# Attention products in 64x64 TensorE tiles, the causal mask moved to VectorE, and a reordered opening, in a DeltaNet and cosine-router kernel

## The chip, the cores and the metric

The kernel runs on one core of one Trainium2 chip. The metric is device time in microseconds of one execution, the median over repeated runs. The profile shows one execution; the times in its rows are counted from the first instruction of that execution.

A core has five engines that run their own instruction streams and wait for each other through semaphores: TensorE (PE in the profile, with its weight loads listed as PEld), VectorE (DVE), ScalarE (ACT), GpSimd (POOL) and SyncE (SP, which here mostly issues DMAs).

## The reference

The first half is a delta-rule linear attention over 4 batches, 8 heads, 768 positions and a head size of 48. The second half is a router that sends each of the 3072 tokens (384 wide, the 8 heads side by side) to one of 8 experts, a two-layer network of width 1024.

```python
k_n = k / (norm(k) + 1e-6)
for t in range(S):
    y[:, :, t] = einsum('bhd,bhde->bhe', q[:, :, t], state)
    v_old = einsum('bhde,bhd->bhe', state, k_n[:, :, t])
    state = state + beta[:, :, t] * einsum('bhd,bhe->bhde', k_n[:, :, t], v[:, :, t] - v_old)
x = y.transpose(0, 2, 1, 3).reshape(B * S, H * D)
logits = (x / norm(x)) @ (emb / norm(emb)).T / tau
e = argmax(logits); gate = softmax(logits)[e]
out = gate * (relu(x @ w1[e]) @ w2[e])
```

All of it is float32.

## The kernel before, in words

**Tiling of the attention.** Positions are cut into 12 chunks of 64 (`m`), and batches into two pairs (`i`). One chunk of one batch pair is a *unit* (`n`, 24 in all); it holds 16 heads as 8 pairs. Inside a chunk the recurrence becomes a triangular system: the kernel builds the Gram matrix of the keys, inverts the 32x32 diagonal blocks of it, and solves for the chunk's updates in two half steps (`solve`, `fix`, `solve_again`), then updates the state (`update`, `new_state`) and forms the output (`from_state`, `inside`). A unit's small products are written with `four(f)`: for each of 4 head pairs, the four corners of the TensorE array, so that one step is 16 calls of `mm`.

**Groups and preparation.** The inverses are made for a *group* of two chunks (four units) at a time, in `prepare(g)`, six groups in all. Its steps: load keys, square and sum them (`square`, `total`), root and scale factors (`roots`, `scales`), scaled keys (`keys`), transpose them (`transposes`, evicted by `out_of_psum`), Gram blocks of the diagonal (`gram_diag`, 64 products of 32x32 a chunk), bring them to lanes (`to_lanes`, a VectorE transpose out of PSUM), clear the upper part (`lower`, GpSimd), then 30 pairs of VectorE operations (`product`, `subtract`, L485 and L489) that do the inversion in every lane at once, `from_lanes`, and `spread` (ScalarE), which writes `W`, the operand of `solve`.

**Per unit, beside the solves.** `gram` (16 products of 64x96) gives the scores; `corner` and `scores` evict them on ScalarE, and `causal` (L582, GpSimd) multiplies them with a mask. After the output, `transposes` (L706) and `xT_out` turn the tokens' rows, `logits` multiplies them with the expert embeddings, and every four units `routing` picks experts, assigns places (`places`), and writes tokens and lists to DRAM.

**Order of the work.** Nothing is in program order by hand: every step is a task for `Plan`, with an engine, an assumed busy time, a due time `key`, and what it reads and writes. `Plan.order` plays the tasks through with these assumed times and emits each engine's stream in the resulting order; on the chip each engine then runs its stream strictly in that order. PSUM is four pairs of banks that tasks take and give back; in `before`, each task that gives a pair back names it with `give`.

**Expert stage.** After the plan, a second part works through the tokens in tiles of 128: `transposed`, `hidden` (L1090), `result` (L1097), with the experts' weights streamed from DRAM. Two such tiles of the first expert (`early_tile`) are already in the plan, late in it.

**Other lines that are named below.** L245 and L248 are the helpers `mm` and `act_copy`, through which most TensorE products and ScalarE evictions go, so they are told apart by tile names. `L432` and `L521` are the transposes of keys and queries, `L470` is `to_lanes`, `L475` is `lower`, `L497` is `from_lanes`, `L600` is `rest`, `L653` and `L651` are `new_state`, `L307` to `L309` load beta.

Of the kernel before, what the change touches and what calls it, by code (L numbers as in the profile page):

```python
# [16 lines left out]
C = 64  # L17
# [5 lines left out]
PERIOD = 7.5  # L23


class Plan:

    def __init__(self, psum):
        self.tasks, self.last, self.readers, self.psum, self.held = [], {}, {}, psum, {}

    def add(self, engine, busy, more, key, run, reads=(), writes=(), take=None, give=None):
        i, after = len(self.tasks), set()
        if take:
            writes = list(writes) + [("psum", take)]
        for r in reads:
            after.update(self.last.get(r, ()))
            self.readers.setdefault(r, []).append(i)
        for w in writes:
            after.update(self.last.get(w, ()))
            after.update(self.readers.pop(w, ()))  # L40
            self.last[w] = [i]
        after.discard(i)
        self.tasks.append((engine, busy, busy + more, key, run, after, take, give))

    def order(self):
# [7 lines left out]
        now, events, serial = 0.0, [], 0  # L53
# [3 lines left out]
        self.span = 0.0  # L57
        self.load = {}
        while len(order) < n:
            for e in sorted(waiting):  # L60
# [5 lines left out]
                i = min(can, key=lambda i: (self.tasks[i][3], i))  # L66
                waiting[e].remove(i)
                _, busy, whole, _, _, _, take, give = self.tasks[i]
                free -= bool(take)
                order.append((now, i))  # L70
                idle[e] = now + busy
# [4 lines left out]
                serial += 2  # L76
            if len(order) == n:
                break
            now = events[0][0]
            while events and events[0][0] <= now + 1e-9:  # L80
                _, _, i = heapq.heappop(events)
                if i < 0:
                    continue
                free += bool(self.tasks[i][7])
                for j in then[i]:
                    missing[j] -= 1
                    ready[j] = max(ready[j], now)
                    if not missing[j]:
                        waiting.setdefault(self.tasks[j][0], []).append(j)
        return order  # L90

    def emit(self):
        free = list(range(len(self.psum)))
        for _, i in self.order():
            _, _, _, _, run, _, take, give = self.tasks[i]
            if take:
                self.held[take] = free.pop(0)
            run()
            if give:
                free.append(self.held[give])  # L100
# [6 lines left out]
def kernel(  # L107
# [22 lines left out]
    WIDE = C  # L130
# [57 lines left out]
    buffers("q", 2, [2, H, WIDE])  # L188
    buffers("v", 3, [2, H, D])
    buffers("sq", 1, [2, H, D])  # L190
    buffers("K", 6, [2, H, WIDE])
# [3 lines left out]
    buffers("rt", 2, [2, 2, NP, 2])  # L195
    rings["X"], rings["WT"] = carved(2, [HC, HC], w2_flat), carved(3, [HC, HC], w2_flat)[2:]
# [45 lines left out]
    HALF = (slice(0, C), slice(C, 2 * C))  # L242

# [9 lines left out]
    half = cpool.tile([128, 2 * GROUP * H], F32, name="half")  # L253
    root = ac.tile([128, 1], F32, name="root")
    bt = rings["XC"][0].rearrange("p g r -> p (g r)")[0:40, 0:NM * 2 * C].rearrange("p (m o t) -> p m o t", m=NM, o=2)
    bt_odd = rings["XC"][1].rearrange("p g r -> p (g r)")[0:40, 0:NM * 2 * C].rearrange("p (m o t) -> p m o t", m=NM, o=2)
# [14 lines left out]
    def pairs_of_heads(t, i, j):  # L271
        return t[:, i, 2 * j:2 * j + 2].rearrange("p h d -> p (h d)")

    def start_constants():
        nc.vector.memset(half, 0.5)
# [6 lines left out]
        for t in rings["K"] + rings["q"]:  # L284
            nc.gpsimd.memset(t[:, :, :, D:WIDE], 0.0)
# [17 lines left out]
    def load_beta():  # L303
        for i in range(2):
            for o in range(2):
                b = beta[2 * i + o].rearrange("(j jj) (m t) -> jj j m t", jj=2, t=C)
                nc.sync.dma_start(out=bt[i * NP:(i + 1) * NP, :, o], in_=b[0])  # L307
                nc.sync.dma_start(out=bt[32 + i * NP:32 + (i + 1) * NP, :, o], in_=b[1])
                nc.sync.dma_start(out=bt_odd[32 + i * NP:32 + (i + 1) * NP, :, 1 - o], in_=b[1])  # L309

    def beta_transposes():
        p = pair("beta")
        for m in range(NM):
            for x, (t, r) in enumerate(((bt, 0), (bt, 32), (bt_odd, 32))):
                nc.tensor.transpose(p[:, min(x, 1), (3 * m + x) * 8:(3 * m + x + 1) * 8],
                                    t[r:r + 8, m].rearrange("p o t -> p (o t)"), ident[r:r + 8, r:r + 8])

    def beta_out():
        p = pair("beta")[:, :, 0:NM * 24].rearrange("p b (m x c) -> p b m x c", x=3, c=8)
        flat = beta_s.rearrange("p m x i j -> p m x (i j)")  # L320
        nc.vector.tensor_copy(flat[:, :, 0], p[:, 0, :, 0])
        nc.vector.tensor_copy(flat[:, :, 1:3], p[:, 1, :, 1:3])

    def newton(r, b, q_):
        nc.vector.tensor_scalar_max(r, r, 1e-30)
        nc.vector.reciprocal(q_, r)
        nc.vector.tensor_tensor(q_, q_, b, op=ALU.mult)
        nc.vector.tensor_tensor(r, r, q_, op=ALU.add)
        nc.vector.tensor_scalar_mul(r, r, 0.5)

    def beta_root(part):
        def step():
            nc.scalar.activation(sqb[:, part], beta_s[:, part], ACT.Sqrt)
        return step

    def beta_newton(part):
        return lambda: newton(sqb[:, part], beta_s[:, part], quot[:, part])
# [6 lines left out]
    def planned_k(m, key):  # L344
        for i in range(2):
            e = nc.scalar if m < 2 and i else nc.sync
            plan.add("ACT" if m < 2 and i else "SP", 2.0, 2.2, key + 0.1 * i,
# [10 lines left out]
    def prepare(g):  # L358
        ms = (2 * g, 2 * g + 1)
        t0 = group_key(g)  # L360
        for m in ms:
            planned_k(m, t0 - 14 * PERIOD + (m % 2) * 2 * PERIOD if m > 1 else -200.0 + m)
        if g == 0:
            plan.add("SP", 1.5, 2.5, -150.0, load_beta, writes=["bt"])
            plan.add("DVE", 1.0, 0.2, -100.0, masks, reads=["iotas"], writes=["masks"])
            plan.add("PE", 2.5, 0.3, -140.0, beta_transposes, reads=["bt", "ident"], take="beta")
            plan.add("DVE", 0.6, 0.2, -140.0, beta_out, reads=[("psum", "beta")], writes=["beta_s"], give="beta")
            for part in (slice(0, 2), slice(2, NM)):
                plan.add("ACT", 0.4, 0.2, -140.0, beta_root(part), reads=["beta_s"], writes=[("sqb", part.start)])
                plan.add("DVE", 1.5, 0.2, -139.0, beta_newton(part), reads=["beta_s"], writes=[("sqb", part.start), "quot"])  # L370
        root_part = ("sqb", 0 if g == 0 else 2)
# [16 lines left out]
        both = [at("rn", g) + (0,), at("rn", g) + (1,)]  # L388
        flat, flat_rt = (t.rearrange("p m i j jj -> p (m i j jj)") for t in (ss, rt))

        def roots():
            nc.gpsimd.tensor_tensor(out=flat_rt, in0=flat, in1=half[:, 0:32], op=ALU.pow)

        def roots_act():
            nc.scalar.activation(flat_rt, flat, ACT.Sqrt)

        def roots_newton():
            nc.vector.tensor_scalar_max(flat_rt, flat_rt, 1e-30)
            nc.vector.tensor_scalar_max(flat, flat, 0.0)
            q_ = quot[:, 0:2].rearrange("p a b c d -> p (a b c d)")[:, 0:32]  # L400
            nc.vector.reciprocal(q_, flat_rt)
            nc.vector.tensor_tensor(q_, q_, flat, op=ALU.mult)
            nc.vector.tensor_tensor(flat_rt, flat_rt, q_, op=ALU.add)
            nc.vector.tensor_scalar_mul(flat_rt, flat_rt, 0.5)
        if g < 2:
            plan.add(*act(32), t0 - 10 * PERIOD, roots_act, reads=both, writes=[at("rt", g)])
            plan.add("DVE", 1.2, 0.2, t0 - 10 * PERIOD, roots_newton, reads=both, writes=[at("rt", g), "quot"])
        else:
            plan.add("POOL", 5.5, 0.2, t0 - 10 * PERIOD, roots, reads=both + ["half"], writes=[at("rt", g)])

        def scales():
            nc.vector.tensor_scalar_add(flat_rt, flat_rt, 1e-6)
            nc.vector.reciprocal(flat_rt, flat_rt)
            for m in ms:
                nc.vector.tensor_tensor(rt[:, m % 2], rt[:, m % 2],
                                        sqb[:, m, 0:3:2].rearrange("p jj i j -> p i j jj"), op=ALU.mult)
        plan.add("DVE", 0.7, 0.2, t0 - 9.6 * PERIOD, scales, reads=[root_part], writes=[at("rt", g)])

        def keys(m):
            def step():  # L420
                for i in range(2):
                    (nc.vector if m == 1 else nc.gpsimd).tensor_tensor(
                        buf("K", m)[:, i, :, 0:D], buf("k", m)[:, i],
# [3 lines left out]
        def transposes(src, m, name):  # L427
            def step():
                p = pair((name, m))
                for i in range(2):  # L430
                    for j in range(NP):
                        nc.tensor.transpose(p[:, i, j * 128:(j + 1) * 128], pairs_of_heads(buf(src, m), i, j), ident)  # L432
            return step

        def out_of_psum(m, name, cols):
            def step():
                act_copy(buf("KQ", m).rearrange("d i j y c -> d (i j y) c")[:, :, cols],
                         pair((name, m)).rearrange("d i (x c) -> d (i x) c", c=C))
# [785 lines left out]
```

## Time and profile before

| What | us |
|---|---|
| median of 14 runs (lowest 661.88, highest 678.58) | 669.91 |
| the profiled execution, its own time | 671.66 |
| its span, first to last instruction | 669.9 |
| first `solve` starts (tile `V`,`W`) | 89.14 |
| fifth `places` starts (tile `run`,`ones`) | 319.61 |
| first TensorE instruction of the expert stage | 368.17 |

The mean granted TensorE clock over the span is 0.868. In the page, "issue" as the reason of an idle time means that the engine waited for nothing that the profile shows. A timeline row merges neighbouring instructions of a kind: start, length, engine, line, operation, tiles, shapes, how many, and in brackets the idle time before it and what ended it.

### The profile page before, as it was taken

How to read it: one execution, taken by the hardware profiler on the slowest of the kernel's cores; microseconds unless marked ns; L12 is line 12 of the kernel's file. 1: busy time of each engine (PE TensorE's matmuls, PEld its weight loads, DVE VectorE, ACT ScalarE, POOL GpSimd, SP SyncE). 2: the span in 40 equal slices, each digit the busy share in tenths (PEclk: the TensorE clock that was granted, in tenths of full speed). 3: DMA queues.
4: the chain of work that ended last, by engine and by line, in shares of the span. 5: the costliest groups of instructions: out<-in, count | busy, mean ns of one | idle time of the engine just before them, and what ended most of it. 6: DMA issues, size and time to landing. Idle time of an engine off the chain costs nothing. (4 is left out here: it accounts for less than half of the span.)

```text
span 669.9 us, 22522 instructions
## 1 busy us (share of the span) xinstructions
PE 560.6 (84%) x9887; PEld 473.4 (71%) x9887; DVE 275.9 (41%) x715; ACT 177.8 (27%) x350; POOL 195.9 (29%) x223
## 2 busy tenths in 40 slices
PE   0364648988787978888997989999999999999992
PEld 0253548887776867788885867878788787878781
DVE  3848998867868967952215101111111111111100
ACT  2232244733534526554341001101010111111010
POOL 2335352647333343333314111212112121212010
PEclk9986555766778869977899889999999999999997
DMA  4444745441231341031201899999999999999700
GB/s 70 82 76 79 195 73 91 74 111 29 39 89 31 64 144 28 10 95 53 79 27 64 292 390 387 370 329 325 316 337 311 335 320 338 308 328 338 234 23 7
DMA packets 129078, 115.49 MB, mean 172 GB/s; under 512 B 84986, under 2 KB 115105, under 8 KB 128978
## 3 DMA queue, kind: packets, MB, share of 16 engines
q1 hardware_dynamic: 122450, 102.98, 50.4%
q0 software_dynamic: 4352, 10.66, 4.3%
q8 instruction: 79, 1.29, 0.8%
q10 hardware_dynamic: 2176, 0.39, 0.4%
q14 instruction: 21, 0.17, 0.1%
HBM read 102.07 MB, written 12.72 MB: 171 GB/s over the span
## 5 line engine op out<-in xcount | busy, mean ns | idle before, releaser
L1092 ACT ACTIVATE hT<-acc 128x512 f32<-128x512 f32 x52 | 31.1, 597 | 261.3 <-PE acc L1090 261.3
L1090 PEld LDWEIGHTS acc<-xTm,w 128*128 128x128 f32 x816 | 93.8, 192 | 4.5
L1090 PE MATMUL acc<-xTm,w 128*128 128x128 f32 x816 | 93.9, 275 | 0.0
L1097 PE MATMUL acc<-w,hT 128*128 128x384 f32 x272 | 92.2, 493 | 0.0
L1100 POOL DMA_INDIRECT out_dram<-y,ids x26 | 26.4, 1014 | 215.1 <-DVE y L1099 197.9
L489 DVE TENSOR_TENSOR w_first<-w_first,tmp 128x30 f32<-128x30 f32 (+9 forms) x180 | 76.5, 427 | 4.5
L485 DVE TENSOR_TENSOR tmp<-w_first 128x30 f32<-128x30 f32 (+9 forms) x180 | 73.3, 409 | 5.8 <-POOL w_first L475 1.4
L1097 PEld LDWEIGHTS acc<-w,hT 128*128 128x128 f32 x272 | 51.1, 193 | 32.4 <-issue 1.7
L1082 DVE COPY xTm<-acc 128x384 f32<-128x384 f32 x26 | 14.5, 558 | 135.2 <-PE acc L1081 131.5
L1099 DVE TENSOR_SCALAR y<-acc,xg 128x384 f32<-128x384 f32 x26 | 16.1, 618 | 126.7 <-PE acc L1097 126.7
L245 PE MATMUL psum_pair<-KQ 48*32 48x32 f32 (+1 forms) x2304 | 50.6, 247 | 21.0 <-issue 17.4
L245 PEld LDWEIGHTS psum_pair<-KQ 48*32 48x32 f32 (+1 forms) x2304 | 41.5, 137 | 28.0 <-issue 22.4
L1090 PEld LDWEIGHTS acc<-xTm,w_first 128*128 128x128 f32 x432 | 51.2, 197 | 3.2 <-DVE xTm L1082 1.0
L582 POOL TENSOR_TENSOR M<-M,upper 128x512 f32<-128x512 f32 x24 | 31.3, 1305 | 73.7 <-ACT M L248 68.3
L1090 PE MATMUL acc<-xTm,w_first 128*128 128x128 f32 x432 | 51.4, 281 | 0.8 <-DVE xTm L1082 0.8
L1097 PE MATMUL acc<-w_first,hT 128*128 128x384 f32 x144 | 47.9, 486 | 0.0
L245 PE MATMUL psum_pair<-S,KQ 48*64 48x48 f32 x1408 | 36.4, 254 | 4.9 <-DVE lz L717 2.1
L1097 PEld LDWEIGHTS acc<-w_first,hT 128*128 128x128 f32 x144 | 26.7, 190 | 16.7
L245 PEld LDWEIGHTS psum_pair<-S,KQ 48*64 48x64 f32 x1408 | 32.1, 169 | 7.4 <-DVE lz L717 2.3
L248 ACT ACTIVATE KQ<-psum_pair 128x1024 f32<-128x1024 f32 x24 | 24.5, 1023 | 36.6 <-PE psum_pair L245 15.5
L1065 POOL DMA_INDIRECT xg<-x_dram,ids x26 | 25.2, 971 | 30.2 <-DMA ids<-idmap 19.6
L542 POOL TENSOR_TENSOR V<-v,sqb 128x384 f32<-128x384 f32 x24 | 20.6, 864 | 34.3 <-DVE R L600 30.9
(181 smaller groups left out, 772.7 us busy)
## 6 DMA issues: line engine op xcount, KB each, us to landing
w<-in_moe_w_dram SPq DMA_DIRECT2D x34, 1536.0 KB
w_first<-in_moe_w_dram SPq DMA_DIRECT2D x16, 1536.0 KB
q<-in_q_dram SPq DMA_DIRECT2D x96, 48.0 KB
v<-in_v_dram SPq DMA_DIRECT2D x48, 96.0 KB
w_first<-in_k_dram SPq DMA_DIRECT2D x88, 48.0 KB
x_dram<-XC SPq DMA_DIRECT2D x5, 800.0 KB
idmap<-space SPq DMA_DIRECT2D x1, 2048.0 KB
w_first<-in_moe_w_dram SPq DMA_DIRECT2D x6, 256.0 KB
```

The source lines that it names most:

```text
L245: nc.tensor.matmul(out_, lhsT=lhsT, rhs=rhs, start=start, stop=True, skip_group_check=True)
L248: nc.scalar.activation(out_, in_, ACT.Copy, scale=scale)
L485: nc.vector.tensor_tensor(t, X[:, j + 1:, j:j + 1].broadcast_to([128, rows, j]), X[:, j:j + 1, 0:j].broadcast_to([128, rows, j]), op=ALU.mult)
L489: nc.vector.tensor_tensor(X[:, j + 1:, 0:j], X[:, j + 1:, 0:j], t, op=ALU.subtract)
L542: nc.gpsimd.tensor_tensor(buf("V", m)[:, i].rearrange("p jj j d -> p jj (j d)").rearrange("p jj (j d) -> p jj j d", d=D), buf("v", m)[:, i ...
L582: nc.gpsimd.tensor_tensor(M, M, K["upper"].broadcast_to([128, H, C]), op=ALU.mult)
L1065: t.read = nc.gpsimd.indirect_dma_start(out=t.x, out_offset=None, in_=x_dram[:, :], in_offset=bass.IndirectOffsetOnAxis(ap=t.ids[:, 0:1], ...
L1090: nc.tensor.matmul(psH[:, i, :], lhsT=t.w1[:, j, (f + i) * 128:(f + i + 1) * 128], rhs=t.xT[:, j, :], start=(j == 0), stop=(j == KC - 1))
L1092: nc.scalar.activation(t.hT[:, f:f + 4, :], psH, ACT.Relu)
L1097: nc.tensor.matmul(psO, lhsT=t.hT[:, f, :], rhs=t.w2[:, f, :], start=(f == 0), stop=(f == NF - 1))
L1099: nc.vector.tensor_scalar_mul(y, psO, t.x[:, Dm:Dm + 1])
L1100: nc.gpsimd.indirect_dma_start(out=out[:, :], out_offset=bass.IndirectOffsetOnAxis(ap=t.ids[:, 1:2], axis=0), in_=y, in_offset=None, bound ...
```

## The change

1. **Products in 64x64 tiles.** Transposes of keys, queries and tokens were transposes of whole 128x128 blocks; they become `mm` products with a 64x64 identity, four corners each (`turned`). The logits, three products over 128 rows, become 12 over 64 rows in two PSUM halves that VectorE adds. The keys are stored without padding between heads (`heads`), beta is transposed by `mm` too.
2. **The mask.** `scores` (ScalarE) and `causal` (GpSimd) become one VectorE operation from PSUM into `M`.
3. **The opening.** Beta is loaded ahead of the second chunk's keys, with 8 DMAs and no second copy; half of that chunk's keys come through the GpSimd queue; roots are refined in 3 operations where there were 5 or 6, separately for chunk 0 and 1; and tasks of group 0 on VectorE are marked `hold`.
4. **The planner.** `hold` lets an engine wait up to `HOLD` for a more urgent task; `mode` and `STAY` make TensorE prefer tasks of the same tile shape; a PSUM pair is free when its last user has been emitted, counted, in place of a named `give`.
5. `from_lanes` writes contiguously, and `spread` reads with a stride in its place.

The core of the diff:

```diff
-    def add(self, engine, busy, more, key, run, reads=(), writes=(), take=None, give=None):
+    def add(self, engine, busy, more, key, run, reads=(), writes=(), take=None, mode=0, hold=False):
...
-                i = min(can, key=lambda i: (self.tasks[i][3], i))
+                i = min(can, key=lambda i: (self.tasks[i][3] + STAY * (e == "PE" and self.tasks[i][8] != mode_now), i))
+                if any(self.tasks[x][9] and now < ready[x] < now + HOLD and self.tasks[x][3] < self.tasks[i][3]
+                       and now + self.tasks[i][1] > ready[x] + 0.1 for x in waiting[e]):
+                    continue
...
-                free += bool(self.tasks[i][7])
+                for a in self.tasks[i][7]:
+                    left[a] -= 1
+                    free += not left[a]
...
+    def turned(p, t):
+        for i in range(2):
+            for j in range(NP):
+                for jj, y in CORNERS:
+                    c = (2 * j + jj) * D
+                    mm(p[HALF[jj], y, (i * NP + j) * C:(i * NP + j + 1) * C], t[HALF[y], i, c:c + C], ident[HALF[y], HALF[y]])
...
-            e = nc.scalar if m < 2 and i else nc.sync
+            e, name, busy = (nc.sync, "SP", 2.2) if m > 1 or not i else (nc.scalar, "ACT", 2.8) if m == 0 else (nc.gpsimd, "POOL", 4.0)
...
-            nc.vector.transpose(WT.rearrange("p x i -> p i x"), X)
+            nc.vector.transpose(WT, X)
...
-            act_copy(M.rearrange("p (jj j) c -> p jj j c", jj=2), split()[:, :, :, HC:])
-
-        def causal():
-            nc.gpsimd.tensor_tensor(M, M, K["upper"].broadcast_to([128, H, C]), op=ALU.mult)
+            nc.vector.tensor_tensor(M.rearrange("p (jj j) c -> p jj j c", jj=2), split()[:, :, :, HC:],
+                                    K["upper"].unsqueeze(1).broadcast_to([128, 2, NP, C]), op=ALU.mult)
...
             for j in range(KC):
-                nc.tensor.transpose(p[:, 0, j * 128:(j + 1) * 128], xrow[:, j * 128:(j + 1) * 128], ident)
+                for a, o in CORNERS:
+                    c = (2 * j + a) * C
+                    mm(p[HALF[a], o, j * C:(j + 1) * C], xrow[HALF[o], c:c + C], ident[HALF[o], HALF[o]])
...
             for j in range(KC):
-                mm(p, buf("xT", n)[:, j], enT[:, j, :], j == 0)
+                for a, o in CORNERS:
+                    mm(p[HALF[o], a, 0:E], buf("xT", n)[HALF[a], j, o * C:(o + 1) * C], enT[HALF[a], j, :], j == 0)
```

## The prediction

> **What bounds the kernel now.** I read the windows first, cut at the three times in the table: the opening, the units, the tail with the early tiles, the expert stage. Columns: stretch, length, busy time (and count) of PE, PEld, DVE, ACT, POOL, granted clock, DMA share, GB/s.
>
> ```profile
> 0.00:89.00 89.00, 36.34 (x1071) 30.80 (x1071) 62.23 (x152) 22.95 (x32) 33.21 (x57) 0.77 0.49 98
> 89.00:320.00 231.00, 195.28 (x6367) 178.21 (x6367) 169.71 (x443) 108.76 (x223) 97.91 (x96) 0.75 0.30 66
> 320.00:368.00 48.00, 42.96 (x709) 35.10 (x708) 13.45 (x69) 15.06 (x44) 14.89 (x20) 0.96 0.18 59
> 368.00:658.00 290.00, 286.03 (x1742) 229.25 (x1742) 30.56 (x52) 31.06 (x52) 48.89 (x51) 0.99 0.87 305
> ...
> 255.00:270.00 15.00, 13.32 (x538) 12.03 (x538) 12.85 (x34) 9.37 (x21) 4.32 (x4) 1.00 0.17 31
> ```
>
> The expert stage is TensorE at 286 of 290 us and unchanged: whatever the attention gains or loses shows one to one at the end. In the units nothing is full: PE 195 of 231, DVE 170. The page gives the clue:
>
> ```profile
> PE 560.6 (84%) x9887; PEld 473.4 (71%) x9887; DVE 275.9 (41%) x715; ACT 177.8 (27%) x350; POOL 195.9 (29%) x223
> ...
> q8 instruction: 79, 1.29, 0.8%
> ```
>
> 19,774 PE instructions against 79 packets on an instruction queue: some 250 a packet. The PE timeline shows when that counts:
>
> ```profile
> 39.66 1.26 PE L245 MATMUL psum_pair<-KQ 48*32 48x32 f32 x108 [1.53 <-issue]
> 40.85 1.09 PE L432 MATMUL psum_pair<-ident,K 128*128 128x128 f32 x8
> 41.87 0.27 PE L245 MATMUL psum_pair<-KQ 48*32 48x32 f32 x11
> 43.50 1.82 PE L245 MATMUL psum_pair<-KQ 48*32 48x32 f32 x128 [1.35 <-issue]
> 47.78 2.54 PE L245 MATMUL psum_pair<-KQ 48*64 48x96 f32 x128 [2.46 <-issue]
> ...
> 89.14 1.11 PE L245 MATMUL psum_pair<-V,W 64*64 64x48 f32 x32 [6.53 <-DVE w_first L470]
> ...
> 152.28 0.83 PE L245 MATMUL psum_pair<-KQ 48*32 48x32 f32 x57 [0.86 <-issue]
> 153.04 1.10 PE L245 MATMUL psum_pair<-Y,Sx 64*64 64x48 f32 x32
> 153.93 1.52 PE L245 MATMUL psum_pair<-KQ 48*64 48x96 f32 x32
> 155.23 0.40 PE L245 MATMUL psum_pair<-U,W 64*64 64x48 f32 x7
> 156.28 0.89 PE L245 MATMUL psum_pair<-U,W 64*64 64x48 f32 x25 [0.65 <-issue]
> ```
>
> Idle times that no engine ended, always 128 matmuls apart: 108+8+11 (one short), 128, and 57+32+32+7. With their weight loads 128 matmuls are 256 instructions, one packet. I call that a page. When PE runs dry a page takes 3.84 (39.66 to 43.50), 4.28 and, in the steady part, 4.00 us (152.28 to 156.28). The busiest 15 us that I found, 255 to 270, ran 538 matmuls: 3.57 us a page. The units average 231/49.7 = 4.65, so PE is already close to its supply.
>
> The opening is VectorE's:
>
> ```profile
> 41.43 1.24 DVE L470 STREAM_TRANSPOSE w_first<-psum_pair 128x1024 f32<-128x1024 f32 x1
> ...
> 46.77 0.29 DVE L485 TENSOR_TENSOR tmp<-w_first 128x130 f32<-128x130 f32 x1
> 52.83 1.25 DVE L470 STREAM_TRANSPOSE w_first<-psum_pair 128x1024 f32<-128x1024 f32 x1 [5.76 <-PE psum_pair L245]
> ...
> 81.58 1.91 DVE L497 STREAM_TRANSPOSE w_first<-w_first 128x1024 f32<-128x1024 f32 x1
> ```
>
> Group 0's inversion runs from 44 to 81.6, stopped for 5.8 us by the next group's `to_lanes` and then shared with that group's steps.
>
> **The change, part by part.** *Opening.* Keys of chunk 0 land about 7 us (the last key load that ScalarE issued, done at 7.63, was followed by its square at 10.99, 3.4 later; now ScalarE's loads end at 3.5). Beta's 8 loads stand behind 4 key loads on SP and end near 6.2; before, PE started 3.2 us after the last of 12, so now at 9.4. VectorE then has, in stream order, two copies (0.6), the sum (0.95), refinements of 3 and 5 small operations (0.85 and 1.0), a scale (0.26): scaled keys start near 14.5, cost 1.65 on GpSimd, PE turns both chunks and ScalarE evicts them (1.0 each) by 21.7. `gram_diag` is 256 matmuls, two pages that must be waited for at 4 us: done near 27. `to_lanes` 1.24, `lower` 1.27 and eight small VectorE operations queued ahead of the first product: 31. Inversion: L485 and L489 take 76.5 and 73.3 us over six groups, 25.0 a group, with 60 gaps of 0.03 (1.8); standing between them in the changed stream two sums, one `to_lanes`, two scales and a copy (3.8): 61.6. One mask (0.7), `from_lanes` 1.25 (contiguous like L470; at worst 1.9 as L497), two `spread` of 1.15: first `solve` at 66 instead of 89.14. It no longer waits for group 2's `to_lanes` to give a pair back; masks that hold pairs end before 66. Load issue that moves to GpSimd (4 loads, about 1 us each by the row of its indirect ones) ends ahead of its first keys. Bounds: 60 to 76.
>
> *Matmul count.* An f32 product leaves two matmuls, a transpose one. Keys and queries: 8 become 64 for each of 24 transposes; tokens 3 become 24, logits 6 become 24, in 24 units. Counted in the emitted streams between first `solve` and fifth `places`, 6364 become 8432 matmuls: 49.7 pages become 65.9. This is the term that decides. Bounds for a page: 3.57 (busiest window) to 4.28 (dry, with the opening's loads). I take 4.00, the dry page of the steady part, since with a third more matmuls for the same work PE will run dry at nearly every page. 65.9 x 4.00 = 263.6, fifth `places` at 66 + 263.6 = 329.6 against 319.6: +10.0.
>
> The Trainium skill speaks against weighing this at all: "Runtime: NRT & Kernel Launch", section "Instruction fetch mechanics", says that instructions come in blocks of 256, prefetched, and that crossing a block is mostly hidden. By it the fetch would cost nothing and the sum would go by PE's work alone, some 50 us better than mine; the stalls at 43.50, 47.78 and 156.28 say that it is not hidden here.
>
> *PE's work itself.* At full clock 16 products of 48 columns take 0.50 us start to start (255.72 to 256.19), those of 96 columns 0.71; 32 of 64 columns are then near 1.13, eight transposes took 0.97: +0.16 a transpose. Logits took 0.77 and become about 0.3; each switch of tile shape costs some 0.13 (0.60 against 0.47 ahead of a transpose). That is about 1 us a unit saved, but under the pages it buys nothing; only in the tail (early tiles, few instructions) it shows: 3 units, -1.5 us, between 0 and -3.
>
> *Mask.* 24 x 0.7 us more on VectorE (R, 384 wide from PSUM, takes 0.55): 17 us on an engine with 61 idle in the units. ScalarE loses 14.2, GpSimd 31.3, whose work ran long ahead of its reader `inside`. Nothing on the path; if VectorE were late, each mask would hold its PSUM pair 0.7 us, 0 to 17 in all. The second logits operation: 24 x 0.16, the same.
>
> *Planner.* `STAY` shifts TensorE tasks by at most 3 us of assumed time; pairs are given back at the same reader or one later. No wait is added that has no cover: 0, from -3 to +5.
>
> Sum: +10.0 - 1.5 = +8.5 on 671.66, 680.2. The profiled execution stands 1.75 above the median: 678.
>
> **Rivals.** *Pages come as fast as in the busiest window* (3.57): 66 + 235.3 = 301.3, -18.3 - 1.5, 650. For it: 538 matmuls in 15 us were real, at clock 1.00. Against: that window still holds stalls by "issue", and what it shows is PE's pace, not the supply with PE always hungry. The sign turns at 3.87 us a page, where 66 + 65.9p is 321.1. Chance 0.28, faster.
>
> *Stalls lower the clock.* Dry PE went with a clock of 0.5 from 60 us on; at that clock 16 products take 0.86 to 0.89, a page 3.5, so each wait for an eviction adds to the page: 4.2 to 4.3, fifth `places` at 343 to 349, 692 to 698. Chance 0.22.
>
> *The opening gains less*: pages for `gram_diag`, beta or queries (PE waits for them in stream order) put the first `solve` at 76: 688. Chance 0.08. Should the masks make VectorE the bound, it is the same size: 17 us more, 695, counted with the clock.
>
> **How the numbers follow.** Forecast 0.42, around 671 to 685. Half a percent, 3.35 us, is about what a measurement of this kernel can tell from no change. Faster than that: the first rival and a little of the forecast (pages at 3.8), 0.31. Within: the forecast's low edge, 0.17. Slower: 0.52. The range goes from the first rival's 650, less its far end, to the clock's 698: 653 to 698.
>
> **What would show it.** Right: more stalls by "issue", 128 matmuls apart, through the units; about 98 packets on the instruction queue (some 12,275 matmuls: 9887 and the 2388 added); first `solve` near 66, 8432 matmuls in 255 to 275 us after it; M on VectorE near 0.7. Wrong: no stalls by "issue" and more than 35 matmuls a us over the units (the page is not the limit); a first `solve` after 76; or VectorE over 14 of 15 us through the units.

## The result, and the profile after

The changed kernel took 711.42 us (median of 10 runs, 703.14 to 714.75) against 669.87: a ratio of 1.065, 95% interval 1.061 to 1.0691. The forecast was 678 in a range of 653 to 698. Here and below a time is the median of all runs of a kernel, and a ratio leaves out its slow ones, over 1.5% above its fastest. The profiled execution took 712.76 us, span 711.0. First `solve` starts at 70.0, fifth `places` at 355.9, expert stage at 408.8 (before: 89.14, 319.61, 368.17).

From the page of the changed kernel, TensorE's counts and its instruction queue; then the windows, cut at these times (columns as before):

```profile
PE 575.9 (81%) x12275; PEld 492.9 (69%) x12275; DVE 265.9 (37%) x773; ACT 180.1 (25%) x327; POOL 165.9 (23%) x203
...
q8 instruction: 98, 1.61, 0.9%
```

```profile
0.00:70.00 70.00, 31.38 (x1235) 28.48 (x1235) 49.99 (x142) 20.02 (x27) 28.14 (x56) 0.82 0.43 76
70.00:356.00 286.00, 211.76 (x8433) 196.88 (x8433) 170.60 (x506) 114.06 (x206) 74.36 (x79) 0.68 0.30 70
356.00:408.70 52.70, 46.78 (x866) 38.25 (x866) 14.79 (x74) 14.97 (x43) 12.76 (x18) 0.88 0.11 35
```

The counts are the forecast ones (12,275 matmuls, 98 packets, 8433 matmuls in the units). The units took 286, not 264, at a mean clock of 0.68 where they had 0.75. VectorE is at 171 of 286: not the bound.

The stalls by "issue" are where they should be. PE's timeline of the changed kernel:

```profile
89.04 1.30 PE L263 MATMUL psum_pair<-KQ 48*32 48x32 f32 x118 [1.27 <-issue]
90.27 0.40 PE L263 MATMUL psum_pair<-enT,xT 64*64 64x8 f32 x10
92.77 0.60 PE L263 MATMUL psum_pair<-enT,xT 64*64 64x8 f32 x14 [2.10 <-issue]
93.30 1.47 PE L263 MATMUL psum_pair<-KQ 48*32 48x32 f32 x114
96.77 0.35 PE L263 MATMUL psum_pair<-KQ 48*32 48x32 f32 x14 [2.00 <-issue]
```

118 + 10 and 14 + 114 are pages of 128 matmuls; they take 3.73 and 4.00 us. I marked every 128th matmul of the units in the trace: of 66 pages 43 end with TensorE dry (idle, with no other engine to wait for), and the 33 that lie between two dry points take 3.83 us in the mean. The 23 that do not end dry take 5.02. The waits of TensorE over the units (engine, line, what it waited for, total, times, longest):

```profile
PE psum_pair L263 <- issue: 54.1, 58, 3.8
PE psum_pair L263 <- ACT W L266: 9.3, 3, 4.5
```

Some 46 of the 54.1 us by "issue" stand at the ends of pages. Before, "issue" was 13.4 us in 26 waits there, and no wait for `W` stood in the list.

One thing has to be known to read the runs: between groups of runs the changed kernel itself differs by 16 us. Its traces differ in two things: stalls of TensorE of another kind, which some groups have and others not (the last section), and the clock over the units (0.68 in the first result, 0.74 in group 4, 0.75 in group 3). How the 16 us divide between them was not separated. Groups are therefore named below, and ratios are to the kernel before within the same group.

### The profile page after: what moved, and what is told of

The parts are those of the page before. It is cut to its first block, busy times and chain, and to the rows that moved or that the text cites. A ratio compares the mean times of both kernels' runs of the same rounds, so it can differ in the third digit from the quotient of the medians.

```text
span 711.0 us, 27346 instructions
## 1 busy us (share of the span) xinstructions
PE 575.9 (81%) x12275; PEld 492.9 (69%) x12275; DVE 265.9 (37%) x773; ACT 180.1 (25%) x327; POOL 165.9 (23%) x203
## 3 DMA queue, kind: packets, MB, share of 16 engines
q1 hardware_dynamic: 122242, 102.93, 47.1%
## 5 line engine op out<-in xcount | busy, mean ns | idle before, releaser
L263 PE MATMUL psum_pair<-KQ 48*32 48x32 f32 (+1 forms) x2304 | 53.4, 261 | 34.0 <-issue 23.3
L263 PEld LDWEIGHTS psum_pair<-KQ 48*32 48x32 f32 (+1 forms) x2304 | 45.1, 150 | 37.6 <-issue 26.8
L534 DVE TENSOR_TENSOR w_first<-w_first,tmp 128x30 f32<-128x30 f32 (+9 forms) x180 | 67.1, 374 | 3.8
L530 DVE TENSOR_TENSOR tmp<-w_first 128x30 f32<-128x30 f32 (+9 forms) x180 | 64.7, 361 | 3.8
L263 PE MATMUL psum_pair<-S,KQ 48*64 48x48 f32 x1408 | 45.9, 271 | 8.4 <-issue 6.8
L263 PEld LDWEIGHTS psum_pair<-S,KQ 48*64 48x64 f32 x1408 | 40.5, 187 | 10.4 <-issue 8.2
L934 POOL DMA_INDIRECT idmap<-tokid,slots_i x24 | 24.3, 1011 | 58.2 <-DVE slots_i L910 21.8
L263 PE MATMUL psum_pair<-ident,XC 64*64 64x64 f32 (+1 forms) x720 | 26.1, 273 | 10.0 <-DMA XC<-in_beta_dram 8.5
```

The lines of the kernel that those rows point to most:

```text
L263: nc.tensor.matmul(out_, lhsT=lhsT, rhs=rhs, start=start, stop=True, skip_group_check=True)
L530: nc.vector.tensor_tensor(t, X[:, j + 1:, j:j + 1].broadcast_to([128, rows, j]), X[:, j:j + 1, 0:j].broadcast_to([128, rows, j]), op=ALU.mult)
L534: nc.vector.tensor_tensor(X[:, j + 1:, 0:j], X[:, j + 1:, 0:j], t, op=ALU.subtract)
L934: put = nc.gpsimd.indirect_dma_start(out=idmap[:, :], out_offset=bass.IndirectOffsetOnAxis(ap=slot_i[:, i:i + 1], axis=0), in_=K["tokid"][ ...
```

## Experiments

Group 1 stood beside 668.08 us of before, group 2 beside 666.39, group 3 beside 664.23, group 4 beside 670.74, group 5 beside 667.95. The extra stalls are in the traces of the first result and of groups 1, 4 and 5, and all but absent in 2 and 3. The changed kernel itself ran in groups 3 and 4 alone. "Matmuls" counts from first `solve` to the expert stage: 7074 before, 9298 after.

### Is it the count? Idle products in the kernel before

```diff
             def step():
                 p = pair((name, m))
+                for _ in range(28):
+                    mm(p[0:32, 0, 0:1], ident[:, 0:32], ident[:, 0:1])
```

and likewise 28 for queries, 10 for tokens, 9 for logits.

> The kernel before, with idle products added and nothing else: ahead of each transposing of keys and queries 28 one-column float32 products (56 matmuls), of tokens 10 (20), of logits 9 (18). From first solve to the expert stage 8826 matmuls instead of 7074; tile shapes, VectorE, planner and opening as before. Theory (instruction supply): the change took 59.7 us more for 2224 more matmuls over that stretch (26.8 ns each), so 1752 more cost about 47 us: 717 us, dry pages as in the changed kernel. Rival (the 64x64 shape, its switches, the mask or the planner cost the time): the added products are tiny, 1752 x 13 ns of PE work or less, 670 to 690 us.

Measured (group 1): 778.08 us, ratio 1.167 (1.1608 to 1.1733). Over twice the expected loss, and not for its reason. TensorE's timeline of this kernel:

```profile
108.26 1.22 PE L245 MATMUL psum_pair<-ident 128*32 128x1 f32 x20 [0.61 <-ACT XC L248]
```

20 idle matmuls over 128 rows hold TensorE 1.16 us (the next row starts at 109.42), 58 ns each; at that price 1752 of them are 101 of the 110 us. TensorE was hardly ever left without instructions: fewer than ten of the 61 pages of the units ended dry. The experiment priced TensorE's own work. The second one uses the tile shape of `gram_diag`:

```diff
+    def idle(p, n):
+        for x in range(n):
+            rows, r = slice(C * (x % 2), C * (x % 2) + D), HC * (x // 2 % 4)
+            mm(p[r:r + HC, x % 2, 0:1], ident[rows, 0:HC], ident[rows, 0:1])
```

> The kernel before with idle products as in the first padded kernel (28, 28, 10, 9 a step), but in 48x32 tiles, two row halves in turn as in gram_diag, one column each, so that they cost TensorE little. 8826 matmuls from first solve to the expert stage, every other step as before. Theory (count alone): as the kernel before with 64x64 forms, 693, dry pages of 3.8 us. Rival (the 64x64 work itself costs the time): 670 to 676.

Measured (group 2): 712.11 us, ratio 1.0649 (1.0554 to 1.0744), +45.7 us. The same place in its timeline:

```profile
102.98 0.37 PE L245 MATMUL psum_pair<-ident 48*32 48x1 f32 x20 [0.61 <-ACT XC L253]
103.29 0.90 PE L714 MATMUL psum_pair<-ident,XC 128*128 128x128 f32 x3
```

Here 20 take 0.31 us to the next start, some 15 ns each: at that price 27 of the 46 us are TensorE's work, the rest is not. 26 ns for each added matmul is what the changed kernel paid too (59.7 us for 2224, 26.8). The rival at 670 to 676 is out: instructions that compute nothing cost time, off any 64x64 tile. But the 693 of the theory was missed by 19, and this pad does not separate supply from work cleanly, since its pages end dry only some 20 times in 61.

### The 64x64 forms alone, and the change without them

The forms in the kernel before, with `heads`, the evictions and the tasks' assumed times that belong to them; mask, opening and planner untouched:

```diff
-                p = pair((name, m))
-                for i in range(2):
-                    for j in range(NP):
-                        nc.tensor.transpose(p[:, i, j * 128:(j + 1) * 128], pairs_of_heads(buf(src, m), i, j), ident)
+                turned(pair((name, m)), buf(src, m))
```

(queries, tokens and logits likewise)

> The kernel before with the 64x64 forms of keys, queries, tokens and logits alone; mask, opening, planner as before. 8850 matmuls from first solve to the expert stage. Theory (instruction supply): as the padded kernel, about 717 us. Rival (planner, PSUM hold or mask are to blame): 665 to 675 us. If it is the tile shape and not the count, this one is near 717 and the padded one near 670.

Measured (group 1): 692.91, ratio 1.0372 (1.0322 to 1.0423): +25 us, neither the +47 of the theory nor the rival's 675 at most. The forms replace 128-row transposes and logits that cost TensorE time of their own, the pads replaced nothing. 44 of its 62 pages end dry; the 30 between two dry points take 3.8 us. The units (columns as above), and TensorE's first wait in them:

```profile
92.00:338.00 246.00, 178.63 (x7963) 164.13 (x7967) 172.81 (x459) 108.58 (x223) 100.03 (x97) 0.81 0.28 63
...
PE psum_pair L246 <- issue: 54.0, 62, 2.4
```

This separates supply from work better than the pads do: TensorE is busy 16 us less than in the kernel before (195 of 231 us), at a higher clock (0.81 against 0.75), and the units still take 15 us longer, with 54.0 us of "issue" where there were 13.4. Beside the changed kernel, in group 4:

> The kernel before with the 64x64 forms alone, now beside the changed kernel: the share of the forms in the whole loss. Theory: 1.035 of before, 25 us, and the changed kernel some 10 us above it, from the mask and the late W, although its first solve is 22 us earlier. Rival: the changed kernel at or under it, and the rest of the change costs nothing.

698.47 us, 1.035 (1.0235 to 1.0465); the changed kernel there 706.85, 1.0564 (1.0482 to 1.0646):

> The changed kernel, as the measure for the next three. 1.05 of before if TensorE's 0.7 us stalls beside the indirect DMAs are absent from its trace (695), 1.065 if they are there (711).

It had the stalls in its trace and lay between the two values expected. So the forms alone lose 25 us, and the whole change loses more although its first `solve` is 22 us earlier. The other way round, the change with 128-row forms (heads padded again, as before):

```diff
-                for jj, y in CORNERS:
-                    c = (2 * j + jj) * D
-                    mm(p[HALF[jj], y, (i * NP + j) * C:(i * NP + j + 1) * C], t[HALF[y], i, c:c + C], ident[HALF[y], HALF[y]])
+                nc.tensor.transpose(p[:, i, j * 128:(j + 1) * 128], t[:, i, 2 * j:2 * j + 2].rearrange("p h d -> p (h d)"), ident)
```

(tokens and logits likewise)

> The changed kernel with keys, queries, tokens and logits back in the 128-row forms; mask on VectorE, new opening and planner kept. 7410 matmuls from first solve (near 68) to the expert stage. Theory (instruction supply): 279 us + 336 x 26.8 ns = 288 us after the first solve, about 658 us, faster than before by some 12. Rival (mask, planner or PSUM hold cost the time): 690 to 711 us.

Measured (group 1): 673.66 us, ratio 0.9988 (0.9943 to 1.0033). Held against the changed kernel's 1.0498 to 1.065 in its three results, the forms cost 5 to 6.6% on top of the rest; but the rest brought nothing, where 12 us less was expected. With tokens and logits alone taken back:

> The changed kernel with tokens and logits alone back in the 128-row forms; keys and queries stay in 64x64. 8362 matmuls from first solve (70) to the expert stage, 936 fewer than in the changed kernel. Theory (instruction supply): 936 x 26.8 ns = 25 us less, 686 us. Rival (keys and queries alone, by their place ahead of the Gram products, cost it): within 5 us of 711; rival (a mechanism other than count): no fixed price for each matmul.

689.98 us, 1.0344 (1.0276 to 1.0411): 21 us less than the changed kernel's first result for 936 matmuls, 23 ns each; by the lower ratios of the changed kernel in groups 3 and 4 it is 10 to 15 us. That is near the 686 expected, and outside the 5 us of the rival that blames keys and queries alone. The price of a matmul is no better known than 11 to 23 ns.

### The parts that the forecast put at nothing

`from_lanes` and `spread` as before; the mask on ScalarE and GpSimd as before; `STAY = 0.0`; one at a time:

```diff
-            nc.vector.transpose(WT, X)
+            nc.vector.transpose(WT.rearrange("p x i -> p i x"), X)
...
-                act_copy(W[:, :, b * HC:(b + 1) * HC], WT.rearrange("p i x -> p x i"), K[name])
+                act_copy(W[:, :, b * HC:(b + 1) * HC], WT, K[name])
```

```diff
-            nc.vector.tensor_tensor(M.rearrange("p (jj j) c -> p jj j c", jj=2), split()[:, :, :, HC:],
-                                    K["upper"].unsqueeze(1).broadcast_to([128, 2, NP, C]), op=ALU.mult)
+            act_copy(M.rearrange("p (jj j) c -> p jj j c", jj=2), split()[:, :, :, HC:])
+        def causal():
+            nc.gpsimd.tensor_tensor(M, M, K["upper"].broadcast_to([128, H, C]), op=ALU.mult)
```

```diff
-STAY = 3.0
+STAY = 0.0
```

> The changed kernel with from_lanes and spread as before (strided write by VectorE, contiguous read by ScalarE). In the changed kernel one spread takes 2.05 us instead of 1.15 and from_lanes 1.24 instead of 1.95, and TensorE waits 9.3 us for W in the units. If the late W adds to the supply of instructions (waits do not overlap with dry pages): two spreads less 1.8, from_lanes more 0.7, 1.1 us for each of the six groups that waits, so 4 to 7 us less, 704 to 707. Rival (only the number of pages counts): 711.

> The changed kernel with the scores evicted by ScalarE and masked by GpSimd as before. Theory (supply, and late W): the mask is covered, 711 within 4 us. Rival (0.7 us on VectorE 24 times delays the inversions, and so W, or holds PSUM pairs): 10 us or more off, at or under 701.

> The changed kernel with STAY = 0: TensorE's tasks are ordered by their due times alone. Theory: the count stays, 711 within 4 us. Rival (the preference for the same shape delays TensorE's urgent steps and costs what the changed kernel has over the kernel before with 64x64 forms alone, 18 us): near 693 to 700.

Measured (group 2): 690.85 (1.0399, 1.0345 to 1.0452), 682.43 (1.024, 1.0178 to 1.0303), 693.12 (1.0425, 1.0377 to 1.0474). Held against 711, each seemed to gain 18 to 29 us. That reading fell with the next group, which had the changed kernel in it:

> The changed kernel again, beside the next three, as their measure: the three kernels with one part undone (lanes, mask, STAY) were each 18 to 29 us faster than it, by runs that did not share a chip with it. If these parts each cost so much: 1.065 of before again, 709 to 713. Rival (the chip of those runs lacks something that the first had, the 0.7 us stalls of TensorE beside GpSimd's indirect DMAs, 18 us in the profile): 1.04 of before, about 695.

> The changed kernel with lanes, mask and STAY all three undone: 64x64 forms, opening and counted PSUM users kept. Sum of the three single gains: 711 - 20 - 29 - 18 = 644, below what the supply of instructions allows. Theory (the bound is the supply of 65.6 pages at 3.83 us and up from the first solve at 68, the three parts only add stalls that keep TensorE from a dry page): 675 to 685, no less. Rival (additive): 645 to 660.

The changed kernel took 694.79 there, 1.0498 (1.0412 to 1.0584), against 1.065 in the first result. The kernel with all three undone took 684.27, 1.0318 (1.0204 to 1.0431); its runs (678.60 to 685.36) all lie under those of the changed one (693.31 to 696.66). The three together cost 10.5 us, within the 675 to 685 expected and far from the additive rival's 660. TensorE's waits by "issue" and for `W` over the units and VectorE's longest, first in the changed kernel of this group:

```profile
PE psum_pair L263 <- issue: 65.1, 48, 3.9
PE psum_pair L263 <- ACT W L266: 8.8, 3, 4.9
...
DVE lz L759 <- PE psum_pair L263: 34.2, 19, 4.6
```

and with the three undone:

```profile
PE psum_pair L263 <- issue: 58.3, 48, 2.5
...
PE psum_pair L263 <- ACT W L266: 2.8, 2, 2.0
...
DVE lz L762 <- PE psum_pair L263: 24.0, 13, 4.2
```

"Issue" keeps its 48 waits and loses 7 us, the wait for `W` loses 6, and VectorE's wait for the logits, behind which the inversions stand in its stream, loses 10. Is it the mask's time on VectorE? It was carried out twice, in the same order (`for _ in range(2):` around it):

> The changed kernel with the mask operation on VectorE carried out twice, in the same stream order: 24 x 0.69 = 16.6 us more on VectorE, nothing else. If the mask costs by VectorE's time (the step of the forecast that put it at nothing fails: inversions and W late): 8 to 16 us more than the changed kernel. Rival (undoing the mask gained 12 to 17 us by another order of the streams, VectorE has cover): within 3 us of the changed kernel.

709.36 us, 1.0583 (1.0468 to 1.0697), against 706.85 of the changed kernel in that group; the runs overlap. 16.6 us more on VectorE cost nothing that can be told, as forecast; by the intervals a few us cannot be excluded. And with the mask kept and the other two undone:

> The changed kernel with lanes and STAY undone, mask on VectorE kept; beside it stands the one with all three undone (1.032 of before). If the mask costs by itself: 1.045 of before, 8 us or more over that one. Rival (each of the three parts is enough to leave an unlucky order): 1.03, within 4 us of it.

699.57 us, 1.0472 (1.038 to 1.0564): 7 us under the changed kernel of its group, near the 1.045 expected if the mask costs by itself. Lanes and `STAY` are then worth 1.0%, all three 1.5% in group 3, which leaves 0.5% for the mask; by group 2, undone alone, it would be over 2%. These do not add, and how the 10.5 us divide stays open. The mask's length does not show as the cause; that another order of the streams is, is what is left, and was only argued.

### The opening alone

128-row forms and lanes as before, mask on VectorE, `STAY` kept; and then mask and `STAY` undone too, which leaves the opening and the counted PSUM users:

```diff
-                    mm(p[HALF[jj], y, (i * NP + j) * C:(i * NP + j + 1) * C], t[HALF[y], i, c:c + C], ident[HALF[y], HALF[y]])
+                nc.tensor.transpose(p[:, i, j * 128:(j + 1) * 128], t[:, i, 2 * j:2 * j + 2].rearrange("p h d -> p (h d)"), ident)
...
-            nc.vector.transpose(WT, X)
+            nc.vector.transpose(WT.rearrange("p x i -> p i x"), X)
```

> The changed kernel with 128-row forms and lanes as before; mask on VectorE, STAY, opening kept. 52.3 pages from first solve to fifth places. Theory (W is late where VectorE ends the inversions late): 5 to 10 us under the kernel with 128-row forms and the new lanes (673.7), 664 to 668, or 0.995 of before. Rival (nothing but the count): as that one, 1.00 of before.

> The kernel before with the new opening and counted PSUM users alone: 128-row forms, lanes, mask and STAY as before. Theory: the first solve at 65 instead of 89 with 7410 instead of 7074 matmuls to come, 9 us of work moved behind it: 655 to 660 us, 0.985 of before. Rival (the opening's gain is given back since VectorE still has five inversions to do and W comes late): 0.995 to 1.005 of before.

Measured (group 3): 653.41, 0.987 (0.9728 to 1.0012), and 650.24, 0.9819 (0.9664 to 0.9975): 11 and 5 us under the times expected. Again, with more rounds, beside the same kernel with `STAY = 3`:

> The opening and the counted PSUM users alone, once more and with more rounds, since its interval reached 0.9975. Theory (the opening's 22 us are kept in part because TensorE has slack between pages where these are only 52): 0.975 to 0.99 of before. Rival (it was faster only where TensorE had no 0.7 us stalls beside the indirect DMAs): 0.995 to 1.005 if these stalls are in its trace.

> The same with STAY = 3. Theory (no 64x64 forms in the units beside 128-row transposes of 3 to 8 instructions, so the preference has little to choose): within 3 us of the one beside it. Rival (it delays TensorE's urgent steps): 5 us or more above it.

Measured (group 5): 659.32, 0.9851 (0.9792 to 0.991), and 663.13, 0.9904 (0.9865 to 0.9942). The opening with the counted PSUM users is faster than both kernels, by 9 to 14 us against the one before, also with the extra stalls in its trace, as the theory had it. The preference for one shape costs it 4 us, more than the 3 expected and less than the rival's 5, with intervals that overlap; mask and preference together cost 3 us in group 3, where the runs overlap too. Its windows in group 3, opening and units:

```profile
0.00:67.00 67.00, 30.91 (x843) 26.25 (x843) 53.30 (x144) 19.74 (x30) 32.15 (x58) 0.84 0.44 79
67.00:297.60 230.60, 196.61 (x6637) 181.68 (x6637) 179.92 (x455) 112.90 (x226) 101.68 (x100) 0.74 0.35 80
```

The first `solve` is 22 us earlier, the units are as long as before (230.6) with 273 more matmuls in them that lay in the opening, and the tail is 48.8: the 22 us arrive whole in that execution. In the medians 14 arrive in group 3 and 9 in group 5; where the rest goes was not followed further.

## Why the prediction was wrong, step by step

**What bounds the kernel: right.** Pages of 128 matmuls, stalls by "issue" a page apart, 98 packets, 12,275 matmuls. The dry page was put at 4.00 and measured 3.83 (33 pages), 3.8 with the forms alone (30), and 3.89 in group 3 (40). That the supply and not TensorE's work lengthens the units is shown by the forms alone.

**The sum over the units: wrong.** 65.9 x 4.00 = 263.6 was to stand for everything in the units. They took 285.9, 4.34 a page, and 277.4 in group 3; this is 22 of the 33 us by which the forecast missed (the tail is 6, the opening 4). The failing sentence is that TensorE "will run dry at nearly every page": 43 of 66 ended dry, the other 23 took 5.02 (in group 3, 16 of 66 at some 4.8). The dry page itself was put too high. 65.9 x 3.83 = 252 is the supply, and by the forecast's own turning point, 3.87 a page, the supply alone would have made the change 3 us faster. What the sum left out are the 33 us above it.

The trace shows what stands there. The 23 pages that do not end dry take 27 us more than 23 x 3.83. In their mean TensorE is busy for 3.97 us and idle for 1.04, 24 us in all: 6.5 for `W`, 7.8 by "issue" away from the ends of pages, the rest mostly for evictions by ScalarE. The granted clock is 0.60 in them and 0.74 in the 43 others, where TensorE is busy for 2.79 us. Two stretches of one page each (the counts take in neighbours at the edges), the first dry at its end, the second not:

```profile
226.99:230.72 3.73, 2.28 (x129) 2.03 (x129) 3.10 (x10) 1.45 (x3) 0.83 (x1) 1.00 0.39 70
242.47:245.86 3.39, 3.39 (x136) 3.39 (x136) 2.86 (x15) 0.70 (x2) 0.00 (x0) 0.50 0.02 5
```

At clock 1.00 the page leaves 1.45 us in which a wait could hide, at 0.50 none. So a wait adds to the time where a page's own work is as long as its supply. How much of the 33 us a full clock would have hidden no experiment tested.

Before, some 35 of 49 pages did not end dry and took 4.9: the waits were in the trace, and I let the page price cover them. Adding all of them would have been too much: before, the units stand 40 us above 49.7 x 3.83 = 190, with the forms alone 8 us (group 1) and 18 (group 4) above 62.3 x 3.83 = 239.

**The parts at nothing: wrong.** "Nothing on the path" for the mask and "No wait is added" for the planner, together with the lanes, cost 10.5 us in group 3. With the three undone, first `solve` to fifth `places` takes 264.3 us. That this is the forecast's 263.6 is luck: it is 252 of supply and 12 above it. For the lanes the mis-sized term is visible. I priced the two `spread` at 1.15 us, the duration of the contiguous read that the change takes away. `W`'s rows, by tile, of the kernel before and of the changed one (shortest/median/longest in ns):

```profile
L248 ACT ACTIVATE W<-w_first,nfirst x6: 1138/1148/1151, 83.5 to 296.3; 128x1024 f32<-128x1024 f32 x6
```

```profile
L266 ACT ACTIVATE W<-w_first,nfirst x6: 2036/2074/2126, 65.9 to 343.8; 128x1024 f32<-128x1024 f32 x6
```

The stride went from VectorE's write (1.95 to 1.24 us) to ScalarE's two reads (1.15 to 2.05 each): 1.1 us later for each `W`, and `W` is what TensorE waits for. The last group of the changed kernel shows it (timeline):

```profile
341.80 0.17 DVE L759 COPY lz<-psum_pair 128x8 f32<-128x8 f32 x1 [0.96 <-PE psum_pair L263]
...
342.52 1.24 DVE L542 STREAM_TRANSPOSE w_first<-w_first 128x1024 f32<-128x1024 f32 x1
...
343.80 2.04 ACT L266 ACTIVATE W<-w_first,nfirst 128x1024 f32<-128x1024 f32 x1 [3.40 <-DVE w_first L542]
...
345.74 1.99 ACT L266 ACTIVATE W<-w_first,nsecond 128x1024 f32<-128x1024 f32 x1
...
347.78 1.96 PE L263 MATMUL psum_pair<-R,W 64*64 64x48 f32 x64 [4.46 <-ACT W L266]
```

VectorE waits for late logits with the end of an inversion queued behind them, then transposes, then ScalarE spreads 4 us, while TensorE stands for 4.46.

**The opening: near.** 70.0 instead of 66. `gram_diag` was done at 27.5 (forecast 27), `from_lanes` at 65.9 (63.5; VectorE waited 3.3 us for a square at 55.5), and the spreads added the missing 1.8.

**The tail: right in group 3.** Forecast 47.1; 47.5 in group 3, 52.9 in the first result, which has stalls of the last section there, at 361 to 364 and 379 to 380. Of TensorE's own work one row was misread: 255.72 and 256.19 lie 0.47 apart, not 0.50; nothing hangs on it.

**The rivals.** The clock's (692 to 698) named the right side and lay nearest. Its mechanism, half the clock, a page's own work of 3.5 us and every wait on top, is what the pages that do not end dry look like, and its 4.2 to 4.3 a page is near the 4.34 measured. Its cause, that dry stalls lower the clock, is not borne out: the forms alone had 0.81 over the units with 44 of 62 pages dry, and 0.71 with some 40 in group 4; the kernel before had 0.75 with some 15 of 49. What sets the clock is open, and no experiment touched it. "Pages at 3.57" is out: dry pages come at 3.83.

The Trainium skill's rule that crossing a block of 256 is mostly hidden ("Runtime: NRT & Kernel Launch", section "Instruction fetch mechanics") does not hold here: some 46 us of "issue" stand at the ends of 43 pages in the units.

## What to carry to other kernels

Count instructions, not only work: where TensorE could issue more matmuls a microsecond than its instruction queue delivers (here 128 in 3.83 us), more and smaller tiles lose even though they lower its work. Pages times the dry page is a floor and not a price. Here the floor was 252 us, the floor with all that stood above it before 292, and the measured units lay between, at 264 (the three parts undone) to 286. When a stride is moved from one engine to another, price the new reader by a strided row, and ask on whose path it lies.

## What the runs showed of the hardware that was not expected

In some groups of runs TensorE issues in bursts while GpSimd carries out an indirect DMA. The changed kernel in the first result:

```profile
307.71 0.48 PE L263 MATMUL psum_pair<-S,KQ 48*64 48x48 f32 x5 [0.42 <-issue]
...
307.74 0.98 POOL L934 DMA_INDIRECT idmap<-tokid,slots_i  x1 [0.21 <-issue]
...
308.47 0.35 PE L263 MATMUL psum_pair<-S,KQ 48*64 48x48 f32 x2 [0.28 <-issue]
```

2 to 8 matmuls each 0.7 us, without a page boundary near. Counted as steps of 0.5 to 0.8 us from one weight load to the next that overlap such a DMA or begin within 1.2 us after it, there are 28 of them (some 18 us, the few matmuls' own work included) from first `solve` to the expert stage in the first trace of the changed kernel, some 30 (some 19 us) in group 4, and at most one in group 3, where the same kernel took 694.79. The kernel before, with 16 (some 10 us) in its trace, varies by 6 us between groups, the changed one by 16. What sets the stalls is open: a group with them (1) and one without (3) ran on the same chip, and no experiment touched the DMAs.
